# A Fourier mix fed into a gated feed-forward block: the opening cut by residue parity, its transposing writes and reads in two halves

## The chip, the core and the metric

The kernel runs on one core of one Trainium2 chip. The metric is the device time of one execution in microseconds. Engines are named as in the profile: PE (TensorE, matrix products), PEld (its weight loads), DVE (VectorE), ACT (ScalarE), POOL (GpSimd) and SP (SyncE, which here only issues transfers). Every operation of the kernel is recorded through one helper, so every profile line says L25 and the groups are told apart by engine and tile name.

## The reference, cut to what matters

```
x: (8, 3008, 256) float32                       # 8 batches
X = fft(fft(x, axis=1), axis=2).real            # along the sequence, then along the 256 channels
t = X.reshape(24064, 256)
g = t @ w_gate;  v = t @ w_val                  # 256 -> 1536, both
out = (gelu(g) * v) @ w_out                     # 1536 -> 256
```

## The kernel before

**The transforms.** The sequence length is 3008 = 64 x 47. Stage one is a product with a 64-point table `G` for each of 24 row groups `jj`; stage two is a 47-point transform for each of 32 residues `g`. Symmetries of real input halve the work: only half of the outputs, `Y` with 1505 columns in an even plane (`eo` 0) and an odd plane (`eo` 1), is formed for each batch, and the mirrored half is had by a change of sign. The channel transform is folded into the first layer's weights: `gen_w` multiplies each 512-wide column block of `w_gate` and `w_val` by a cosine and sine table `CW` and gives `WE` (even), `WOP` (odd) and `WOM` (odd times minus two).

**Stage one** is `a_step(b, k)`, 12 steps per batch: two products of 256 columns into one PSUM bank, which ACT or DVE copies to `S1`. `z_write` sends `S1` to a buffer `z` in device memory and `z_read` reads it back, transposed, in three thirds into `Ap`. Before stage one, `fold_x` adds and subtracts mirrored channels of the loaded `x`: on DVE for batch 0, on POOL for the others.

**Stage two** is `b_steps(b, eo, q)`: eight products of 47 columns for each quarter `q` of the residues, with `Ap` as weights, and copies from PSUM to `Y`. In batch 0 the odd plane has eight more for its row 0. Stage two of later batches runs in one PSUM bank, `ps_d`, of which there is one; so do most `a_step` and some `gen_w`.

**The main loop** runs over units `u`, 36 for each batch: three chunks of `Y` columns (`CH`: 481, 512, 512 columns) by 12 feed-forward groups of 128. A unit makes the gate and the value for its columns and for the mirrored ones: five first-layer products (`WE`, `WOP`, for the gate also `WOM`), six in the first chunk of batch 0. ACT applies Gelu (`glp`, `glm`), DVE and POOL multiply into `h`. From the end of unit 12 on, eight or six second-layer products (`ps_o`, `Wo_sb`) for the chunk before are run per unit, and `finish` copies and stores their rows.

**The order** of each engine is the program's order, since every engine is wrapped in `_InOrder`: a waiting instruction holds whatever is behind it on its engine. Around the loop the order is written by hand: `extra` (which unit makes which late weight block, casts it on POOL with `cast_w`), `a_first` (which unit makes which stage-one step of batch 1), `first`, `evens` and `later` (stage two of the next batch). In a unit, `fills` are stage-two products put between the unit's own products, two at a time, and `tail` is their copy to `Y`.

**The opening** of batch 0, before unit 0: loads of `x` and of the first weight block; the table `G`; `fold_x` and `a_step` with dummy products (`warm`) between; five `z_write`; three `z_read`; the late weight blocks and batch 1's `x`; the first weight block (`cast_w(0)` on POOL, `gen_w(0, ...)`); the stage-two tables (`cols_t`, `phase_t`, `sin_t`); the load of the Gelu table; dummy products that wait for a small read `gate`; then all eight `b_steps` and unit 0.

The lines that set the order in the units:

```
extra = {1: [lambda: cast_w(1024)], 13: [gen_tf]}
for n, turn in ((0, (ps_o, ps_d, ps_o, ps_d)), (1, (ps_o, ps_o, ps_d, ps_o))):
    for j, bank in enumerate(turn):
        extra.setdefault(4 * n + j, []).append(
            lambda f0=512 + 512 * n, i=1 - j // 2, eo=j % 2, bank=bank: gen_w(f0, i, eo, bank))
a_first = {4: (0,), 5: (1,), 12: (10,), 13: (11,), 14: (12,), 15: (13,)} | {
    8 + j: (2 + 2 * j, 3 + 2 * j) for j in range(4)}
```

Of the kernel before, what the change touches and what calls it, by code (L numbers as in the profile page):

```python
# [9 lines left out]
FP32 = mybir.dt.float32  # L10
# [27 lines left out]
def kernel(  # L38
# [34 lines left out]
    CH = [(1024, NCOL - 1024), (0, 512), (512, 512)]  # L73
    MID = 24
# [26 lines left out]
    lone = const_pool.tile([128, NFC], BF16)  # L101

# [92 lines left out]
    def z_tile():  # L195
        return dram.tile([HJ, 128, C], BF16, tag="z", bufs=2, name="z")
# [14 lines left out]
    def fold_x(b, i, eng, a0=0, an=8, other=None):  # L211
        xt = xins[i]
        o0 = (8 * i + a0) * C
        lo = _sub(xt, [[C, an], [1, 127]], a0 * C + 1)
        hi = _sub(xt, [[C, an], [-1, 127]], a0 * C + 255)
        ea = _sub(xf, [[C, an], [1, 127]], o0 + 1)
        od = _sub(xf, [[C, an], [1, 127]], o0 + 129)
        eng.tensor_tensor(ea, lo, hi, op=ALU.add)
        eng.tensor_tensor(od, lo, hi, op=ALU.subtract)
        (other or eng).tensor_copy(  # L220
            _sub(xf, [[C, an], [128, 2]], o0), _sub(xt, [[C, an], [128, 2]], a0 * C))
# [25 lines left out]
    def cols_t():  # L247
        f4, f8, f16 = (col_q[:, i : i + 1] for i in range(3))
        vec.tensor_scalar(col_q, col_q, MAGIC, None, op0=ALU.add)
        vec.tensor_scalar(col_q, col_q, MAGIC, None, op0=ALU.subtract)  # L250
        vec.scalar_tensor_tensor(col_t, f4, -4.0, col_p, op0=ALU.mult, op1=ALU.add)
        vec.scalar_tensor_tensor(col_bot, f8, -2.0, f4, op0=ALU.mult, op1=ALU.add)
        vec.scalar_tensor_tensor(f8, f16, -2.0, f8, op0=ALU.mult, op1=ALU.add)
        vec.scalar_tensor_tensor(col_j, col_t, 8.0, f16, op0=ALU.mult, op1=ALU.add)
        vec.scalar_tensor_tensor(col_j, f8, 24.0, col_j, op0=ALU.mult, op1=ALU.add)
        vec.tensor_scalar(col_j, col_j, 1.0 / N2, None, op0=ALU.mult)
        for o, b0 in ((0, 0.25), (2 * N2, 0.0)):
            vec.tensor_scalar(
                _sub(quat, [[1, 2 * N2]], o), _sub(col_bot, [[0, 2 * N2]], 0),
                0.25, b0, op0=ALU.mult, op1=ALU.add)  # L260
        vec.tensor_scalar(col_k, col_t, 3.0, None, op0=ALU.is_lt)
        vec.tensor_scalar(col_w, col_k, -TWO_PI, None, op0=ALU.mult)
        vec.tensor_tensor(col_bot, col_bot, col_k, op=ALU.mult)
        vec.tensor_tensor(col_top, col_k, col_bot, op=ALU.subtract)

    TO = 4 * N2
    iota(_sub(rowt, [[2 * N2, 2], [1, 2 * N2]], 0), [[0, 2], [1, 2 * N2]], 0, 0)
    iota(_sub(rowt, [[NJ, 2], [1, MID]], TO), [[0, 2], [1, MID]], 0, 0)
    iota(_sub(rowt, [[NJ, 2], [1, MID - 1]], TO + MID), [[0, 2], [1, MID - 1]], 1, 0)
    pool.memset(_sub(rowt, [[NJ, 2]], TO + NJ - 1), 0.0)  # L270
    pool.memset(_sub(quat, [[1, NJ]], TO), 0.25)
    pool.memset(_sub(quat, [[1, NJ]], TO + NJ), 0.0)
    TG = TO + 2 * NJ
    iota(_sub(rowt, [[NG, 2], [1, NG]], TG), [[0, 2], [-11, NG]], 0, 0)
    pool.memset(_sub(quat, [[1, NG]], TG), 0.25)
    pool.memset(_sub(quat, [[1, NG]], TG + NG), 0.5)
# [59 lines left out]
    def sin_g(i):  # L336
        for h in range(2):
            act.activation(
                _sub(G, [[128, 8], [1, 64]], i * 8 * 128 + h * 64),
                _sub(reds[i], [[64, 8], [1, 64]], 0), AF.Sin, scale=col_h[h][:, :])  # L340

    def turn_g():
        for r, to, of, n, sign in ((0, 0, 0, 16, 1.0), (2, 2, 2, 16, -1.0), (1, 1, 33, 8, 1.0),
                                   (1, 33, 1, 8, -1.0), (3, 3, 35, 8, -1.0), (3, 35, 3, 8, 1.0)):
            pat = [[128, 8], [64, 2], [4, n]]
            act.activation(_sub(G, pat, 16 * 128 + to), _sub(G, pat, of), AF.Copy, scale=sign)
# [44 lines left out]
    def cast_w(f0):  # L391
        big = work.tile([128, 2, NCH, 512], BF16, tag="ev" if f0 == 1024 else "dv", bufs=2, name="wb")
        for i in (1, 0):
            wb[(f0, i)] = big[:, i, :, :]
            pool.tensor_copy(wb[(f0, i)], wst[0][:, i, :, f0 : f0 + 512])

    def gen_w(f0, i, eo, bank):
# [6 lines left out]
        if eo == 0:  # L404
            on_half(ps, act.activation(WE[:, i, fs], ps, AF.Copy))
        else:
            on_half(ps, act.activation(WOP[:, i, fs], ps, AF.Copy))
            on_half(ps, vec.tensor_scalar(
                WOM[:, i, fs], ps, col_m, None, op0=ALU.mult))
# [22 lines left out]
    def n_turn(b):  # L432
        pool.tensor_tensor(
            NA[:, :, :], _sub(Ap, [[0, 2], [C, NG]], 128), TB[:, :, :], op=ALU.mult)
# [27 lines left out]
    def a_step(b, k):  # L462
# [6 lines left out]
        else:  # L469
            ps = ps_o() if b == 1 and k % 2 and 1 < k < 10 else ps_d()  # L470
# [10 lines left out]
    def z_write(b, j0, nj, eng=sync):  # L481
        if "z" not in st[b]:
            st[b]["z"] = z_tile()
        z, S1 = st[b]["z"], st[b]["S1"]
        dst = ap_replace(
            z[0:1, 0, :], ap=[[C, 128], [128 * C, nj], [1, C]], offset=z[j0, 0:1, :].offset)
        eng.dma_start(out=dst, in_=_sub(S1, [[C, nj], [1, C]], j0 * C))

    def z_read(b, third):
        z = st[b]["z"]  # L490
        src = ap_replace(
            z[0:1, 0, :], ap=[[NG * C, 32], [1, NG * C]], offset=z[8 * third, 0:1, :].offset)
        p_step = Ap[:, :, :].ap[0][0]
        dst = ap_replace(
            Ap[:, :, :], ap=[[4 * p_step, 32], [1, NG * C]],
            offset=Ap[:, :, :].offset + third * p_step)
        sync.dma_start(out=dst, in_=src)

    def b_steps(b, eo, q):
# [3 lines left out]
        def mm(gi, m1):  # L503
            def run():
                if "ps" not in box:
                    box["ps"] = ((ps_o, ps_d, ps_vh, ps_vh) if eo else (ps_vh, ps_g) * 2)[q]() \
                        if b == 0 else ps_d()
# [474 lines left out]
```

## Time and profile before

| | |
|---|---|
| median of 3 runs | 631.53 us (631.25 to 631.95) |
| the profiled execution | 629.75 us |
| its span on the core | 627.6 us |
| PE busy | 606.0 us, 97% |
| DVE busy | 541.5 us, 86% |
| ACT busy | 471.8 us, 75% |
| POOL busy | 449.7 us, 72% |
| moved by transfers | 82.39 MB, mean 131 GB/s |

Times in the profile count from the start of the span. In a timeline row the first number is the start, the second how long the row lasts; a group of several instructions in a row overlaps in time where the engine is pipelined. "[x <-A t]" means that the engine sat idle for x before the row and that a result of engine A in tile t ended it. SPq is the queue of SP; its rows are the issuing of transfers, not the transfers. In a table of stretches the columns are the length, then busy time and instruction count of PE, PEld, DVE, ACT and POOL, the granted clock, the share of transfer engines busy and GB/s.

### The profile page before, as it was taken

To read this page: it belongs to the slowest core of one execution; us is meant where nothing else is said; L and a number is where in the kernel's file an instruction comes from. 1 tells how busy PE (TensorE), PEld (TensorE's weight loads), DVE (VectorE), ACT (ScalarE), POOL (GpSimd) and SP (SyncE) were. 2 spreads that over 40 slices of the span, in tenths; PEclk is the share of its full clock that TensorE was granted. 3 is DMA by queue.
4 is the path that set the end of the run, shared out by engine and by line. 5 is a ranking of instruction groups with operands and counts; after the bars stand their busy time and mean duration, and the time that the engine had idled before them with its cause. 6 is when DMAs were issued, how large, how long until landed. Compare 5 with 4: busy or idle time off the path is not lost.

```text
span 627.6 us, 12916 instructions
## 1 busy us (share of the span) xinstructions
PE 606.0 (97%) x4522; PEld 402.0 (64%) x4580; DVE 541.5 (86%) x654; ACT 471.8 (75%) x956; POOL 449.7 (72%) x480
## 2 busy tenths in 40 slices
PE   3899999999999999999999999999999999999997
PEld 2445666766666666766667666666667666666665
DVE  7688988898888998888988898889898898999991
ACT  8687778877788777877778777887778777766662
POOL 8296987769868789687787788687885555556552
PEclk9999999999999999999999999999999999999999
DMA  8997523653237512574246533366223612222113
GB/s 311 348 283 234 153 64 113 173 185 98 76 101 218 194 49 74 177 223 121 51 119 173 190 103 74 104 208 204 56 60 93 194 45 50 60 50 52 39 47 85
DMA packets 65458, 82.39 MB, mean 131 GB/s; under 512 B 8298, under 2 KB 58986, under 8 KB 62578
## 3 DMA queue, kind: packets, MB, share of 16 engines
q1 hardware_dynamic: 63682, 80.65, 42.4%
q0 software_dynamic: 1552, 0.79, 0.9%
q8 instruction: 36, 0.59, 0.4%
q14 instruction: 28, 0.23, 0.1%
q10 hardware_dynamic: 160, 0.13, 0.1%
HBM read 45.08 MB, written 37.25 MB: 131 GB/s over the span
## 4 chain that ended last, share of the span: by engine, by line
PE 91%; DMA 3%; DVE 3%; ACT 1%; issue 1%; POOL 0%; SPq 0%; ACTq 0%; DVEq 0%; POOLq 0%
PE ps_o L25 38%; PE ps_g L25 28%; PE ps_v L25 19%; PE ps_d L25 6%; DMA xin<-in_x_dram 3%; DVE h L25 1%; DVE S L25 0%; DMA z<-S 0%; ACT glp L25 0%; DVE xf L25 0%; ACT glm L25 0%; ACT S L25 0%; POOL xf L25 0%; SPq L25 0%; DVE WOM L25 0%
## 5 line engine op out<-in xcount | busy, mean ns | idle before, releaser
L25 POOL TENSOR_TENSOR h<-glm,dv 128x1024 bf16<-128x1024 bf16 (+1 forms) x138 | 290.9, 2108 | 153.2 <-DVE dv L25 110.0
L25 PE MATMUL ps_o<-Wo_sb,h 128*128 128x256 bf16 x2136 | 277.7, 272 | 0.5 <-DVE S L25 0.3
L25 DVE SCALAR_TENSOR_TENSOR ev<-nq,WN,ps_v 128x512 f32<-128x512 bf16 (+1 forms) x276 | 202.6, 734 | 62.3 <-PE ps_v L25 43.5
L25 ACT ACTIVATE glm<-ps_g 128x512 bf16<-128x512 f32 (+1 forms) x288 | 169.4, 588 | 110.0 <-PE ps_g L25 70.8
L25 PEld LDWEIGHTS <-h 128*128 128x128 bf16 x2208 | 210.8, 97 | 54.6 <-issue 0.9
L25 ACT ACTIVATE glp<-ps_g 128x512 bf16<-128x512 f32 (+1 forms) x288 | 169.9, 590 | 9.9 <-PE ps_g L25 0.3
L25 DVE TENSOR_TENSOR h<-glp,ps_v 128x1024 bf16<-128x1024 bf16 (+2 forms) x150 | 172.9, 1153 | 4.9 <-ACT glp L25 2.7
L25 DVE SCALAR_TENSOR_TENSOR dv<-ev,ps_v 128x1024 f32<-128x1024 f32 (+1 forms) x138 | 164.8, 1194 | 0.0
L25 POOL TENSOR_TENSOR xf<-xin 128x254 bf16<-128x254 f32 x168 | 118.3, 726 | 1.8 <-DMA xin<-in_x_dram 1.8
L25 PE MATMUL ps_g<-Y,WOM 128*128 128x512 bf16 (+1 forms) x288 | 107.7, 374 | 0.3
L25 PE MATMUL ps_v<-Y,WOP 128*128 128x512 bf16 (+1 forms) x288 | 107.7, 374 | 0.0
L25 PE MATMUL ps_v<-Y,WE 128*128 128x512 bf16 (+1 forms) x282 | 105.7, 375 | 0.1
L25 PE MATMUL ps_g<-Y,WOP 128*128 128x512 bf16 (+1 forms) x278 | 103.9, 374 | 1.7
L25 PE MATMUL ps_g<-Y,WE 128*128 128x512 bf16 (+1 forms) x249 | 92.9, 373 | 0.0
L25 PEld LDWEIGHTS <-WOP 128*128 128x128 bf16 x576 | 55.7, 97 | 52.8 <-ACT WOP L25 0.4
L25 PEld LDWEIGHTS <-WE 128*128 128x128 bf16 x576 | 56.0, 97 | 30.9 <-issue 0.6
L25 ACT ACTIVATE osb<-ps_o 128x512 f32<-128x512 f32 x93 | 54.8, 589 | 17.6 <-PE ps_o L25 13.6
L25 PEld LDWEIGHTS <-Ap 128*128 128x128 bf16 (+1 forms) x561 | 40.9, 95 | 33.8 <-issue 0.2
L25 ACT ACTIVATE S<-ps_d 128x512 bf16<-128x512 f32 x80 | 47.4, 593 | 0.1
L25 PEld LDWEIGHTS <-G 128*128 128x128 bf16 x213 | 20.8, 100 | 33.2 <-issue 11.8
L25 ACT ACTIVATE Y<-ps_d 128x192 bf16<-128x192 f32 (+4 forms) x142 | 34.0, 340 | 0.5 <-PE ps_d L25 0.5
L25 PEld LDWEIGHTS <-WOM 128*128 128x128 bf16 x300 | 29.2, 97 | 4.9
(140 smaller groups left out, 262.7 us busy)
## 6 DMA issues: line engine op xcount, KB each, us to landing
out_dram<-osb SPq DMA_DIRECT2D x358, 64.0 KB
xin<-in_x_dram SPq DMA_DIRECT2D x16, 1024.0 KB
Ap<-z SPq DMA_DIRECT2D x24, 512.0 KB
xin<-in_x_dram SPq DMA_DIRECT2D x8, 896.0 KB
z<-S SPq DMA_DIRECT2D x7, 768.0 KB
z<-S SPq DMA_DIRECT2D x8, 512.0 KB
nq<-nrow SPq DMA_DIRECT2D x8, 376.2 KB
z<-S SPq DMA_DIRECT2D x11, 256.0 KB
```

The costliest lines, as they stand in the source:

```text
L25: return lambda *a, **k: self._tc.keep_in_program_order(call(*a, **k))
```

## The change

Residues are handled by parity. `G`'s columns are reordered so that the even residues come out on partitions 0 to 63 of `S1` and the odd ones on 64 to 127. There are two device buffers, `z0` and `z1`, and `z_write` and `z_read` take `halves`. `Ap` holds the 16 even residues first.

In the opening, only the even half is written and read ahead of the loop (five writes of 64 partitions, then three reads); the odd half follows as one write behind the 512 weight block, its reads behind batch 1's first `x` load, and the 1024 block behind these. Only quarters 0 and 1 of stage two run ahead of unit 0. Quarters 2 and 3 (the odd residues) run as fills of units 5 to 8, all in `ps_d`. For batch 0 the first chunk is 512 columns made of even residues alone (`CH0`), the second the 481 columns of both, the third 512 columns of odd residues. Their rows lie two apart in the output, so `store_apart` stores them window by window, and a copy `aside` keeps the columns that would otherwise share a window.

Residue 0 is split into two products of 24 and 23 columns, one in each of quarters 0 and 1, in every batch; the copies to `Y` are two per quarter instead of two to four. In all batches `z` is written and read in two halves.

Other moves: the constants of the channel table are made early on POOL, the small constants of `cols_t` move from DVE to POOL, the single-channel copies of `fold_x` of batch 0 all go to POOL, `cast_w(0)` from POOL to DVE, two copies of first weight blocks from ACT to DVE, `WOM` is made from `WOP` instead of from PSUM; the dummy products between stage-one groups and the `gate` read are gone. The 1024 block is cast three units in, instead of one, its four `gen_w` all use `ps_o`; `load_wo` moves from before the loop to unit 5, `n_first(0)` from unit 0 to unit 8. Stage one of batch 1 runs from unit 8 to unit 17 instead of 4 to 13, and its last read is issued in unit 18 instead of 15.

```
+    CH0 = [(0, 512), (1024, NCOL - 1024), (512, 512)]
...
-    def z_write(b, j0, nj, eng=sync):
+    def z_write(b, j0, nj, halves=(0, 1)):
         if "z" not in st[b]:
-            st[b]["z"] = z_tile()
...
+            st[b]["z"] = [z_tile(half) for half in range(2)]
+        S1 = st[b]["S1"]
+        for half in halves:
+            z = st[b]["z"][half]
+            dst = ap_replace(
+                z[0:1, 0, :], ap=[[C, 64], [64 * C, nj], [1, C]], offset=z[j0, 0:1, :].offset)
+            sync.dma_start(out=dst, in_=_sub(S1, [[C, nj], [1, C]], j0 * C, 64 * half, 64))
...
-                    box["ps"] = ((ps_o, ps_d, ps_vh, ps_vh) if eo else (ps_vh, ps_g) * 2)[q]() \
-                        if b == 0 else ps_d()
+                    box["ps"] = ((ps_o, ps_d) if eo else (ps_vh, ps_g))[q]() \
+                        if b == 0 and q < 2 else ps_d()
...
+        def store_apart(w, t, s):
+            part = lambda p0, n: _sub(t, [[1, C]], s * C, p0, n)
+            if isinstance(w[2], tuple):
+                row, nb = w[2]
+                nc.sync.dma_start(
+                    out=ap_replace(
+                        out, ap=[[64 * C, nb], [2 * C, 16], [1, C]], offset=out.offset + row * C),
+                    in_=part(0, 16 * nb))
...
-        warm((5, 2, 10)[i])
-    z_read(0, 0)
-    z_read(0, 1)
-    gate = work.tile([128, 128], BF16, tag="gate", bufs=1, name="gate")
...
-    z_read(0, 2)
+    warm(7)
+    z_read(0, 0, (0,))
+    z_read(0, 1, (0,))
+    z_read(0, 2, (0,))
     for i in (1, 0):
         load_w(512, i)
+    z_write(0, 0, HJ, (1,))
     load_x(1, 0)
+    for i in range(3):
+        z_read(0, i, (1,))
     for i in (1, 0):
         load_w(1024, i)
...
     for eo in range(2):
-        for q in range(4):
+        for q in range(2):
...
-    load_wo()
-    extra = {1: [lambda: cast_w(1024)], 13: [gen_tf]}
-    for n, turn in ((0, (ps_o, ps_d, ps_o, ps_d)), (1, (ps_o, ps_o, ps_d, ps_o))):
+    extra = {3: [lambda: cast_w(1024)], 5: [load_wo], 13: [gen_tf]}
+    for n, turn in ((0, (ps_o, ps_d, ps_o, ps_d)), (1, (ps_o, ps_o, ps_o, ps_o))):
         for j, bank in enumerate(turn):
-            extra.setdefault(4 * n + j, []).append(
+            extra.setdefault(4 + j if n else (1, 2, 2, 3)[j], []).append(
...
-    a_first = {4: (0,), 5: (1,), 12: (10,), 13: (11,), 14: (12,), 15: (13,)} | {
-        8 + j: (2 + 2 * j, 3 + 2 * j) for j in range(4)}
+    a_first = {8: (0, 1), 9: (2, 3), 18: (13,)} | {10 + j: (4 + j,) for j in range(8)}
...
+    second_half = {5: (0, 2), 6: (0, 3), 7: (1, 2), 8: (1, 3)}
...
+                if b == 0 and i in second_half:
+                    steps, tail, _, _ = b_steps(0, *second_half[i])
+                    fills += steps
```

## The prediction

> **What bounds the kernel now.** I read the page first, then the table of stretches, then the timelines of PE, POOL and SP over the first 75 us, where all that is moved lies.
>
> ```profile
> span 627.6 us, 12916 instructions
> PE 606.0 (97%) x4522; PEld 402.0 (64%) x4580; DVE 541.5 (86%) x654; ACT 471.8 (75%) x956; POOL 449.7 (72%) x480
> ```
>
> ```profile
> 3.50:9.50 6.00, 0.62 (x4) 0.46 (x5) 5.58 (x8) 5.48 (x14) 4.79 (x16) 1.00 1.01 418
> 17.50:18.50 1.00, 0.97 (x4) 0.19 (x2) 0.93 (x6) 0.64 (x2) 0.00 (x0) 1.00 0.96 291
> 36.47:53.30 16.83, 15.30 (x101) 7.76 (x101) 15.51 (x28) 13.54 (x28) 16.83 (x39) 1.00 0.75 196
> 53.30:78.00 24.70, 24.49 (x176) 15.81 (x179) 22.26 (x26) 18.20 (x37) 19.03 (x22) 1.00 0.67 210
> ```
>
> From 53.3 us on PE is full (24.49 of 24.70). So what is won or lost before then, plus any new PE wait behind it, is the whole effect. Loads move 418 GB/s, the transposing writes about 300.
>
> ```profile
> 8.88 0.58 PE L25 MATMUL ps_g<-xf,G 128*128 128x256 bf16 x2 [8.88 <-DVE xf L25]
> 12.46 0.38 PE L25 MATMUL ps_g<-xf,G 128*128 128x256 bf16 x2
> ...
> 23.60 1.90 PE L25 MATMUL ps_d<-G,gate 128*128 128x512 bf16 x8 [2.30 <-DMA gate<-z]
> 28.60 0.38 PE L25 MATMUL ps_v<-Y,WE 128*128 128x481 bf16 x1
> 29.17 0.36 PE L25 MATMUL ps_g<-Y,WOP 128*128 128x481 bf16 x1
> 36.47 0.59 PE L25 MATMUL ps_o<-wb,CW 128*128 128x512 bf16 x2
> 37.70 0.37 PE L25 MATMUL ps_v<-Y,WE 128*128 128x481 bf16 x1
> 53.30 1.03 PE L25 MATMUL ps_o<-Wo_sb,h 128*128 128x256 bf16 x8 [0.25 <-DVE S L25]
> 70.45 0.19 PE L25 MATMUL ps_d<-T0Q,Ap 128*128 128x47 bf16 x2
> ```
>
> The first two rows show the pace of PE (below). The others are my milestones: unit 0 at 28.60, the 1024 block's first product (end of unit 4) at 36.47, unit 5 at 37.70, the first second-layer product (end of unit 12) at 53.30, stage two of batch 1 (unit 21) at 70.45.
>
> ```profile
> 31.77 1.40 POOL L25 TENSOR_TENSOR xf<-xin 128x254 bf16<-128x254 f32 x2 [1.80 <-DMA xin<-in_x_dram]
> 33.25 2.00 POOL L25 CAST wb<-wst 128x1024 bf16<-128x1024 f32 x2
> 35.22 1.40 POOL L25 TENSOR_TENSOR xf<-xin 128x254 bf16<-128x254 f32 x2
> ```
>
> POOL waits for batch 1's first `x` (31.77), folds once, casts the 1024 block by 35.25: just ahead of PE.
>
> ```profile
> 19.88 0.45 SPq L25 DMA_DIRECT2D Ap<-z  x1
> 56.56 0.37 SPq L25 DMA_DIRECT2D z<-S  x1
> 63.50 0.48 SPq L25 DMA_DIRECT2D Ap<-z  x1
> 66.80 1.22 SPq L25 DMA_DIRECT2D xin<-in_x_dram  x2
> ```
>
> The last opening read is issued at 19.88. For batch 1 the last write goes at 56.56, its read at 63.50, three units ahead of need and before the next `x`.
>
> **Part by part: the opening.** DVE's folds end at 13.67 as before. Without dummies the last stage-one copy ends near 16.3 (before 16.65). Then DVE: `reduce_c` 1.7 us (16.56 to 18.22), two casts, `phase_t` 1.4 (20.16 to 21.58). The trace has no DVE cast of 1024 elements: from below, its single-input rows (256 elements 0.32 apart, 512 0.46) extend to 0.74; from above, the fold of 1016 takes 1.22. I take 0.74, the nearer kind; the other end costs 1.0, covered as shown below. `cols_t` on POOL (16 instructions at 0.24, after two 1.8 us memsets) ends near 18.7, beside this. ACT: `sin_t` 1.1, Gelu table 1.3. Half of stage two is 1.7 us on PE. Unit 0's third product comes at about 24.5 instead of 29.17: **a lead of 4.6 us.**
>
> **The lead meets the 1024 block.** PE then needs units 0 to 4: 0.45 us to the end of unit 0, four units of six products of 0.2165 (1.3 us) and four weight blocks of 0.43, and some tenths of waits, so it asks for the 1024 block at 32.3. What POOL has by then depends on batch 1's first `x`. In its queue stand, from 18.8 (first read back, 2 us after issue): three half reads 0.79 MB to 21.0, 1.05 MB of weights to 23.5, the odd write 0.79 MB at 300 GB/s to 26.1, the `x` 1.05 MB at 418 to 28.6. Before, the landing that POOL saw trailed the mean rate by up to 2 us; I take 1.1: 29.7. Bounds: 28.1 (writes overlap reads) and 31.6 (as before). Then come **three** folds of 1.5 us instead of one, and the cast, 1.0: PE resumes at 35.3, unit 5 starts at 35.75. Against 37.70: **-1.95 us**, between -3.5 and -0.05. PE idles 3 us here, so up to 3 us lost or gained in the opening itself changes nothing: this covers the edits there that I cost at zero (casts, `cols_t`, single-channel copies, dummies, `gate`). If the cover were gone, they would cost what they last.
>
> **Units 5 to 12, the odd half in one bank.** PE work: units 5 and 6 with 8 stage-two products (0.2) and a weight block, 1.95 each; unit 7 with 16 (0.6), a block and `gen_wn` (0.6), 2.93; unit 8 with 16 and two stage-one steps of 0.22, 2.34; then 1.74, 1.52, 1.52 and 1.27 up to the first second-layer product: 15.2. The waits come on top. Fills start right behind a unit's value products, while the one `ps_d` still holds the previous quarter. In unit 5 Gelu ends 2.0 after its start; DVE then has two multiplies (0.6 each) queued ahead of the copies to `Y` (0.35 and 0.25 from the 192-element rows of 0.27): free at 3.9. PE is there at 2.4: **1.5**. Unit 7's fills wait for ACT's copies: **0.2**. Behind unit 7, `gen_wn` wants `ps_d` at 8.0 and DVE, again two multiplies first, frees it at 9.6: **1.6**. Unit 8's stage-one step waits for ACT's copies: **0.8**. Sum 19.3; before, 53.30 - 37.70 = 15.6. So **+3.7**, between -0.4 (no wait shows) and +4.5. What is queued behind is all of PE's first layer, and Gelu and DVE behind that. `WOM` from SBUF instead of PSUM (a 264-element row takes 0.29, the old one 0.75) frees DVE, which isn't late at those points.
>
> **Stage one of batch 1.** Five steps instead of one remain behind unit 12: 4 x 0.22 = +0.9. In units 12 to 23 the products are 481 wide instead of 512: 60 x 0.013 = -0.8. Together **+0.1**. Two of its copies now lie on DVE there (1.2 us, DVE has 2.4 idle in 24.7). The last write goes at the end of unit 17 + 0.2; before, such bytes took 2.1 us and 0.6 to be seen. SP then issues two stores, the next `x` and only then the read. The `x` (0.98 MB, 2.3 us) is ahead in the queue; two half reads take 1.5 and 0.5 to land: 7.9 after unit 17. PE wants them after three units of 1.67 and 0.8: 5.8. **+2.1**, between 0.5 and 3.2.
>
> [...]
>
> **All batches.** Two more products in each of 7 batches, at 0.026 (8 take 0.205): **+0.36**. Six more transfers per batch cost SP about 0.5 each, beside long SP waits; from batch 2 on the reads have five units, not three. ACT loses one short copy per plane. `aside` on POOL takes 1.5 (copies of 512 and 256 elements take 0.62 and 0.41) for 1.2 removed, in a unit where POOL waits for DVE anyway. `n_first` at unit 8 has four units for two transfers: they need 3 us each on a quiet queue and come just in time; 7.7 us, what the first waited in the old crowd, would stall PE by up to 4. I take 0 because the transfer engines were only 0.38 busy from 45.5 to 53.3.
>
> **Sum:** -1.95 + 3.7 + 0.1 + 2.1 + 0.36 = **+4.3 us**. The profiled span of 627.6 goes to 631.9, its execution of 629.75 to 634.1; the median, 1.8 above that execution, from 631.53 to **635.8**.
>
> **The rivals.**
> - *Not slower: the one bank costs nothing.* If DVE frees `ps_d` before PE asks (copies done within 1.1 us of the last product, instead of 2.6), the 4.1 us of waits are gone: 631.7. For it: in units 5 to 12 before, DVE was busy 15.5 of 16.8 and PE waited little. Against: the copies stand behind multiplies that wait for Gelu.
> - *The late read lands in time*, if the next `x` doesn't hold it up: 633.7. With the first rival: 629.6, faster.
> - *The clock drops.* PE idles about 3 us in unit 4. The trace shows products at half pace from 8.9 to 12.5 us (a pair of 256 columns every 0.43, later every 0.22), and none such after the idle 2.30 ahead of the `gate` products. If the longer gap brings that pace back for as long, 3.6 us, 1.8 is lost: 637.6. [...]
> - *The lead never arises* (tables late): until 3 us are lost the end is the forecast's.
>
> **How the numbers follow.** Forecast 0.60, one bank free 0.14, read in time 0.12, clock 0.08, both waits gone 0.06. Faster by over 0.2% (1.26 us, about what a measurement of this kernel can tell) is the last case and the lower fifth of the second: 0.09; the rest of the second is within: 0.11; slower 0.80. Range 631.9 to 639.3: below lies 0.13; above, a landing as late as before (+1.9) with both waits at their upper ends, 0.06.
>
> **What would show it.** Right: unit 0 near 24.1; PE idle about 3 us ahead of the 1024 block, ended by POOL's `wb`; waits on DVE's `Y` in units 6 and 7; an idle of about 2 us ahead of batch 1's stage two, ended by the read of `z`. Wrong: a weight block cast before PE asks, second-layer products starting before 53, or no wait at unit 21.

## The result and the profile after

The changed kernel takes 654.39 us (median of four runs, 645.36 to 654.88) against 631.39 us for the kernel before in the same session: a ratio of 1.033, 95% interval 1.024 to 1.042. It is slower, as forecast, but by 23 us where 4.3 were forecast, and far above the range. The profiled execution took 654.52 us. Two single executions of the experiments, one with the dummy products (656.12 us) and one of the mended kernel with the load in unit 5 (640.25 us), fell into a slower state of the chip, and the medians leave them out.

The page's head and busy times of the changed kernel:

```profile
span 652.7 us, 12997 instructions
PE 614.8 (94%) x4581; PEld 403.8 (62%) x4581; DVE 548.9 (84%) x643; ACT 475.5 (73%) x943; POOL 455.8 (70%) x491
```

The span grew by 25.1 us, while PE is busy for 8.8 us more (614.8 against 606.0) with only 59 more products. So PE both waits longer and works more slowly. The milestones of the prediction, in the timeline of PE of the changed kernel:

```profile
25.17 0.61 PE L25 MATMUL ps_v<-Y,WE 128*128 128x512 bf16 x1
37.77 1.01 PE L25 MATMUL ps_o<-wb,CW 128*128 128x512 bf16 x2 [3.83 <-POOL wb L25]
38.58 0.63 PE L25 MATMUL ps_v<-Y,WE 128*128 128x512 bf16 x1
43.69 0.22 PE L25 MATMUL ps_d<-TP,Ap 128*128 128x47 bf16 x2 [0.32 <-DVE Y L25]
53.88 0.58 PE L25 MATMUL ps_v<-Y,WOM 128*128 128x512 bf16 x1 [7.05 <-DVE h L25]
68.97 1.04 PE L25 MATMUL ps_o<-Wo_sb,h 128*128 128x256 bf16 x8
93.60 0.24 PE L25 MATMUL ps_d<-TQ,Ap 128*128 128x47 bf16 x2 [7.05 <-DMA Ap<-z]
```

| stage | before | after | difference | forecast |
|---|---|---|---|---|
| opening, to unit 0 | 28.60 | 25.17 | -3.4 | -4.6 |
| units 0 to 4, to unit 5 | 9.10 | 13.41 | +4.3 | +2.65 |
| units 5 to 12, to the second layer | 15.60 | 30.39 | +14.8 | +3.7 |
| units 12 to 21, to stage two of batch 1 | 17.15 | 24.63 | +7.5 | +2.2 |
| the rest | 557.15 | 559.10 | +1.95 | +0.36 |

(The third forecast is the rest of the prediction's -1.95 for both first rows.) Three idle gaps of PE stand out: 3.83, 7.05 and 7.05 us. Behind each of them the products come at half their pace. The table of stretches of the changed kernel, one stretch behind each gap (length, then busy time and count of PE, PEld, DVE, ACT, POOL, granted clock, transfer share, GB/s):

```profile
37.77:43.40 5.63, 5.60 (x20) 1.90 (x19) 1.58 (x4) 2.36 (x4) 5.30 (x9) 0.50 0.87 320
53.80:60.50 6.70, 6.07 (x57) 2.64 (x57) 3.48 (x10) 1.86 (x4) 0.15 (x2) 0.50 0.01 2
93.60:98.00 4.40, 4.40 (x24) 2.40 (x24) 1.63 (x2) 1.93 (x4) 1.85 (x4) 0.50 0.05 8
```

The granted clock is 0.50 in all three: in the first two, 512-column products start 0.43 us apart, and in the third 481-column ones 0.40, where they start 0.22 and 0.20 apart at a granted clock of 1.00. At full clock the same work would last half of 5.60 + 6.07 + 4.40 us, so 8.0 us are lost to the clock. The opening has a fourth such stretch: from 22.1 to 26.4 us, behind an idle of 1.52 us, the granted clock was 0.60.

What ends the first gap of 7.05 us is a product that waits for DVE, and DVE was held by a single instruction, in its timeline:

```profile
43.55 9.68 DVE L25 TENSOR_SCALAR WOM<-WOP,col_m 128x512 bf16<-128x512 bf16 x1
```

The other five of these products take 0.34 to 0.73 us. POOL at that time, and ahead of it, in its timeline:

```profile
31.56 1.46 POOL L25 TENSOR_TENSOR xf<-xin 128x254 bf16<-128x254 f32 x2 [5.12 <-DMA xin<-in_x_dram]
36.68 1.04 POOL L25 CAST wb<-wst 128x1024 bf16<-128x1024 f32 x1 [0.48 <-DMA wst<-in_moe_w_val_dram]
...
42.09 1.28 POOL L25 DMA_DIRECT2D Wo_sb<-in_moe_w_out_dram  x1
43.39 1.41 POOL L25 TENSOR_TENSOR xf<-xin 128x254 bf16<-128x254 f32 x2
...
52.36 1.44 POOL L25 TENSOR_TENSOR xf<-xin 128x254 bf16<-128x254 f32 x2
```

The first two rows belong to unit 4: `x` landed at 31.56, not at 29.7, and when its three folds were done the weights themselves were still 0.48 us away. The last three rows: POOL issues the `Wo` load and then folds without a gap, and the held product ends at 53.23, within the last fold.

Why the weights were so late stands in the chain of waits of the changed kernel (start, length, what):

```profile
19.82 7.87 DMA z<-S
30.34 6.29 DMA wst<-in_moe_w_val_dram
```

The odd half's write, issued at 19.82, was done at 27.69. SP waited 4.9 us for it with the odd half's reads, and the weights stand behind these in its order: they were issued at 30.34 and landed 6.29 us later. At unit 21, the queue of SP:

```profile
81.63 1.31 SPq L25 DMA_DIRECT2D z<-S  x2
83.04 2.72 SPq L793 DMA_DIRECT2D out_dram<-osb  x2
85.85 1.25 SPq L25 DMA_DIRECT2D xin<-in_x_dram  x2
87.20 1.18 SPq L25 DMA_DIRECT2D Ap<-z  x2
```

The read is issued 5.6 us behind the last write, after two stores and the next `x`, and PE gets its data at 93.60.

### The profile page after: what moved, and what is told of

Its sections match the earlier page's. It is cut to its first block, busy times and chain, and to the rows that moved or that the text cites. A ratio compares the mean times of both kernels' runs of the same rounds, so it can differ in the third digit from the quotient of the medians.

```text
span 652.7 us, 12997 instructions
## 1 busy us (share of the span) xinstructions
PE 614.8 (94%) x4581; PEld 403.8 (62%) x4581; DVE 548.9 (84%) x643; ACT 475.5 (73%) x943; POOL 455.8 (70%) x491
## 4 chain that ended last, share of the span: by engine, by line
PE 89%; DMA 5%; DVE 3%; SPq 1%; ACT 1%; issue 0%; POOL 0%; ACTq 0%; DVEq 0%
PE ps_o L25 37%; PE ps_g L25 28%; PE ps_v L25 18%; PE ps_d L25 6%; DMA z<-S 2%; DVE WOM L25 1%; DMA xin<-in_x_dram 1%; DMA wst<-in_moe_w_val_dram 1%; DMA Ap<-z 1%; SPq L25 1%; DVE h L25 1%; DVE xf L25 0%; ACT glp L25 0%; DVE S L25 0%; SPq L793 0%
## 5 line engine op out<-in xcount | busy, mean ns | idle before, releaser
L25 PE MATMUL ps_v<-Y,WE 128*128 128x512 bf16 (+1 forms) x288 | 109.2, 379 | 0.0
L25 PE MATMUL ps_g<-Y,WOP 128*128 128x512 bf16 (+1 forms) x288 | 108.7, 378 | 0.0
L25 PE MATMUL ps_g<-Y,WE 128*128 128x512 bf16 (+1 forms) x288 | 108.5, 377 | 0.0
L25 PEld LDWEIGHTS <-Ap 128*128 128x128 bf16 (+1 forms) x578 | 45.5, 99 | 58.4 <-issue 22.0
L25 ACT ACTIVATE osb<-ps_o 128x512 f32<-128x512 f32 x93 | 55.2, 594 | 17.8 <-PE ps_o L25 12.8
L25 ACT ACTIVATE Y<-ps_d 128x192 bf16<-128x192 f32 (+4 forms) x133 | 41.5, 408 | 0.7 <-PE ps_d L25 0.7
L25 PE MATMUL ps_d<-xf,G 128*128 128x256 bf16 x166 | 31.8, 273 | 1.6 <-DVE S L25 0.8
```

The source lines that it names most:

```text
L25: return lambda *a, **k: self._tc.keep_in_program_order(call(*a, **k))
```

## The experiments

Each kernel was measured beside runs of the kernel before on the same chip. Since that one's median moved between 630.12 and 631.47 us, I compare the excess over it: +23.0 us for the change.

### What holds DVE's product

**First: the product read from PSUM again.**

```
             if f0:
-                minus_two()
+                on_half(ps, vec.tensor_scalar(
+                    WOM[:, i, fs], ps, col_m, None, op0=ALU.mult))
```

> The changed kernel, with the late minus-two weights (WOM above column 512) read from PSUM again. Theory A (the one 9.68 us product WOM<-WOP on VectorE was held because it reads and writes SBUF while GpSimd issues the Wo load): no WOM takes over 0.8 us, TensorE's 7.05 us wait at 53.88 us goes, and the half-rate stretch at 50 to 60 us (about 3.2 us) goes with it: 654.4 - 10.3 = about 644 us (642 to 647). Theory B (the wait is only passed on, since the longer PSUM reads hold the one bank): 650 us or more, with waits on ps_o in units 3 to 6. Theory C (the clock falls for another reason than this wait): the wait goes and the slow stretch stays, about 647.5 us.

646.62 us, +16.5, in theory A's range. No `WOM` takes over 0.75 us, the 7.05 us wait and the half pace behind it are gone. But the next DVE operation with both sides in SBUF is now the long one, in the timeline of DVE of this kernel:

```profile
49.89 3.16 DVE L25 CAST WN<-WNb 128x12 f32<-128x12 bf16 x1
```

It writes 12 columns. The multiplies into `h`, which read PSUM, ran through the same 10 us at 0.67 to 0.69 us each. So it isn't the product that matters, but that it works from SBUF to SBUF.

**Second: the load three units later.**

```
-    extra = {3: [lambda: cast_w(1024)], 5: [load_wo], 13: [gen_tf]}
+    extra = {3: [lambda: cast_w(1024)], 8: [load_wo], 13: [gen_tf]}
```

> The changed kernel, with the Wo load issued at unit 8 instead of unit 5, when all WOM products are done. Theory A (the Wo load on GpSimd holds the product): all six WOM products under 1 us, 643 to 647 us, unless another SBUF-to-SBUF operation of VectorE near unit 8 is held in its stead for up to 9 us (then 650 to 654 us, and the long operation stands beside the Wo load again). Theory B (GpSimd's folds, which run back to back there, hold it): one WOM product still takes over 5 us, 652 to 655 us.

651.77 us, +21.7. That is within the 650 to 654 us that theory A gave for another held operation, but a `WOM` product was held: the expectation took all products to be done by unit 8's place in POOL's queue, which they weren't. POOL got there at 45.80, ahead of the last product. That gives the clearest pair of rows, DVE first, then POOL, both in their timelines:

```profile
42.78 0.87 DVE L25 TENSOR_SCALAR WOM<-WOP,col_m 128x512 bf16<-128x512 bf16 x1
48.41 4.05 DVE L25 TENSOR_SCALAR WOM<-WOP,col_m 128x512 bf16<-128x512 bf16 x1
```

```profile
45.80 1.28 POOL L25 DMA_DIRECT2D Wo_sb<-in_moe_w_out_dram  x1
...
51.59 1.44 POOL L25 TENSOR_TENSOR xf<-xin 128x254 bf16<-128x254 f32 x2
```

Folds ran at both times. The product ahead of the load got through in 0.87 us, the one behind it was held to 52.46, again within the last fold. In this kernel, the changed one and the one with the product from PSUM, the held operation ends 0.87, 0.87 and 0.74 us behind the start of the last fold, and 6.7 to 11.1 us behind the load's issue. The end follows the folds, not the load.

**Third: one part of the change alone, in the kernel before.**

```
-            on_half(ps, vec.tensor_scalar(
-                WOM[:, i, fs], ps, col_m, None, op0=ALU.mult))
+            if f0:
+                vec.tensor_scalar(WOM[:, i, fs], WOP[:, i, fs], col_m, None, op0=ALU.mult)
+            else:
+                on_half(ps, vec.tensor_scalar(
+                    WOM[:, i, fs], ps, col_m, None, op0=ALU.mult))
```

> The kernel before, with only this part of the change: WOM above column 512 made from WOP in SBUF instead of from PSUM. Theory A (held by the Wo load, which is issued at 28.7 us there and moves its data at about 33 to 43 us): one of the products at 33.0, 36.7, 40.8 us takes several us, and the time goes to 635 to 642 us. Theory B (the folds hold it, or the product is only held at unit 5 of the changed kernel): four products of about 0.35 to 0.7 us, 631 us within 0.7.

630.39 us, ratio 1.000 (0.998 to 1.002): no cost, and theory A in this form (the load in flight is enough) has fallen. The operations of DVE on this tile:

```profile
L25 DVE TENSOR_SCALAR WOM<-WOP,col_m x4: 348/583/945, 35.0 to 45.8; 128x512 bf16<-128x512 bf16 x4
```

The first three ran while `Wo` was still moving (issued at 29.36, landed 15.2 us later), and all four beside folds. What differs is that POOL here runs dry behind the load, 0.42 us ahead of the next fold and 0.82 us behind that one, before its long run of folds begins. New theory: the load must be followed by folds without a gap.

**Fourth: the load behind the last fold.**

```
-    extra = {3: [lambda: cast_w(1024)], 5: [load_wo], 13: [gen_tf]}
+    extra = {3: [lambda: cast_w(1024)], 12: [load_wo], 13: [gen_tf]}
```

> The changed kernel, with the Wo load issued on GpSimd at unit 12, behind the last of its folds, instead of at unit 5, between folds. Theory A (a VectorE operation that works from SBUF to SBUF is held from a Wo load that is directly followed by folds until the folds end): no WOM product and no WN copy above 1 us, TensorE's 7.05 us wait goes; the Wo data lands near 64 us, which is when the first second-layer product can start: 644 to 648 us. Theory B (the folds alone, run back to back, hold it): one WOM product or the WN copy still takes 3 to 10 us, 650 to 655 us.

647.97 us, +17.8, in theory A's range. No `WOM` over 0.91 us: the folds alone hold nothing. PE pays for the late load instead, in its timeline:

```profile
62.37 1.86 PE L25 MATMUL ps_o<-Wo_sb,h 128*128 128x256 bf16 x8 [2.37 <-DMA Wo_sb<-in_moe_w_out_dram]
```

The eight products last 1.86 us, where such a group takes 1.04 at full clock: half pace again, behind a gap of 2.37 us.

**Fifth: both ingredients in the kernel before**, that is, the third experiment and

```
-    load_wo()
-    extra = {1: [lambda: cast_w(1024)], 13: [gen_tf]}
+    extra = {1: [lambda: cast_w(1024)], 5: [load_wo], 13: [gen_tf]}
```

> The kernel before, with the late WOM made from SBUF (no cost by itself) and its Wo load moved behind unit 4's fold, so that folds stand directly ahead of it and behind it. Theory A (load, then folds without a gap, hold VectorE's SBUF-to-SBUF operations until the last fold): one WOM product or the WN copy after about 42 us takes 3 to 8 us, TensorE waits 2 to 6 us for it, 633 to 640 us. Theory B (something else of the changed kernel is needed): no such operation over 1 us, 630 to 632 us.

640.49 us, ratio 1.014 (1.011 to 1.016), just above theory A's range. Timelines of DVE, POOL and PE of this kernel:

```profile
38.59 0.71 DVE L25 TENSOR_SCALAR WOM<-WOP,col_m 128x512 bf16<-128x512 bf16 x1
42.10 9.78 DVE L25 TENSOR_SCALAR WOM<-WOP,col_m 128x512 bf16<-128x512 bf16 x1
```

```profile
40.79 1.24 POOL L25 DMA_DIRECT2D Wo_sb<-in_moe_w_out_dram  x1
...
51.02 1.44 POOL L25 TENSOR_TENSOR xf<-xin 128x254 bf16<-128x254 f32 x2
```

```profile
52.51 0.56 PE L25 MATMUL ps_v<-Y,WOM 128*128 128x480 bf16 x1 [8.37 <-DVE h L25]
```

The same picture without the rest of the change: short ahead of the load, 9.78 us behind it, free within the last fold. The PE wait was 8.37 us, more than the 2 to 6 expected.

**Sixth: POOL made to run dry once behind the load**, by a copy of one column that waits for the product (the copied column is not used).

```
+    extra[5].append(lambda: pool.tensor_copy(lone[:, 0:1], WOM[:, 1, 1024:1025]))
     extra[7].append(gen_wn)
```

> The changed kernel, with one copy on GpSimd behind the Wo load that waits for unit 5's WOM product, so that GpSimd runs dry between the load and the next folds. Theory A (only folds that follow the load without a gap hold VectorE): unit 5's product takes under 1 us, and the WOM and WN of unit 7 under 1 us too: 644 to 648 us. [...] Mixed: unit 5's product is short, unit 7's operation is held by the folds that follow, 646 to 652 us.

646.24 us, +15.9, theory A. DVE, then POOL, in their timelines:

```profile
43.30 0.34 DVE L25 TENSOR_SCALAR WOM<-WOP,col_m 128x512 bf16<-128x512 bf16 x1
48.93 0.96 DVE L25 TENSOR_SCALAR WOM<-WOP,col_m 128x512 bf16<-128x512 bf16 x1
```

```profile
43.71 0.19 POOL L25 COPY lone<-WOM 128x1 bf16<-128x1 bf16 x1 [0.69 <-DVE WOM L25]
```

The load stands where it stood, and the same seven folds follow. One pause of 0.69 us sets DVE free, and the folds behind the pause hold nothing (0.96 and, for the `WN` copy, 0.51 us). So the load alone doesn't hold DVE either, since unit 5's product took 0.34 us while the data was on its way (issued at 41.73, landed 8.8 us later); the unbroken run of POOL behind it does. In the time this gap is worth 23.0 - 15.9 = 7.1 us. That is less than its 7.05 us of wait and 3.0 of half pace, because other waits show once it is gone: 1.29 and 1.51 us on copies to `Y`, and 8.30 instead of 7.05 at unit 21.

Where POOL ran no load directly ahead of its folds, the `WOM` products from SBUF took 0.34 to 0.98 us, so what was held there was less than one fold instruction, 0.7 us (half of the fold row's 1.41). Behind the load the wait was 9.3 us in the changed kernel, through 13 such instructions and six small casts. Why the run behind a load keeps DVE out to its end, no run here shows.

### What delays unit 21

**Stage one of batch 1 two units earlier**, two steps a unit in units 8 to 11 with the second in `ps_o`, the last read in unit 16:

```
-            ps = ps_o() if b == 1 and k in (1, 3) else ps_d()
+            ps = ps_o() if b == 1 and k in (1, 3, 5, 7) else ps_d()
...
-    a_first = {8: (0, 1), 9: (2, 3), 18: (13,)} | {10 + j: (4 + j,) for j in range(8)}
+    a_first = {8: (0, 1), 9: (2, 3), 10: (4, 5), 11: (6, 7), 16: (13,)} | {12 + j: (8 + j,) for j in range(4)}
```

> The changed kernel, with stage one of batch 1 finished at unit 15 instead of 17 (two steps a unit at units 8 to 11) and its last read at unit 16. If the delay of stage one is what makes the wait at unit 21: that wait of 7.05 us falls to 0 to 1 us, the half-rate stretch of 2.2 us behind it goes, and the two steps more a unit cost up to 0.8 us each in two units: 654.4 - 9 + 1 = about 646 us (644 to 648). If something else makes it (the rate of the 64-partition transfers, whenever they start): 4 us or more of the wait stay, 650 us or more.

646.25 us, +16.1: as expected. The last read is issued at 82.32, and PE's first product of that stage runs at 85.75 with no wait. The delay of stage one costs 23.0 - 16.1 = 6.9 us.

**The next `x` behind the read:**

```
-            loads = (0, 14, 19) if b else (8, 12, 18)
+            loads = (0, 14, 19) if b else (8, 12, 19)
```

> The changed kernel, with the third x load of batch 2 issued behind the last z read of batch 1 instead of ahead of it. If the place in the sync queue sets stage two's wait at unit 21: the wait of 7.05 us shrinks by the 1.25 us of the issue and about 2 us of the x transfer to about 3.8 us, and with a gap that short the half-rate stretch at 91 to 98 us (about 2.2 us) may go too: 649 us (647 to 652). If the output stores alone hold the read: the wait stays at 5.8 us or more, the slow stretch stays, 653 us (652 to 654.5).

650.88 us, +20.8, in the first theory's range. In PE's timeline of this kernel:

```profile
90.84 0.21 PE L25 MATMUL ps_d<-TQ,Ap 128*128 128x47 bf16 x2 [2.76 <-issue]
```

The wait is 2.76 us (3.8 expected) and the products behind it run at full pace. The `x` load ahead of the read thus made 4.3 us of the 7.05. For the other 2.76 us the row names no engine; that they are the read itself, issued too late, is argued from the kernel above, where an earlier read leaves no wait.

### What delays unit 5

**The 1024 block's weights ahead of the odd reads and `x`, its cast ahead of the folds:**

```
-    load_x(1, 0)
-    for i in range(3):
-        z_read(0, i, (1,))
     for i in (1, 0):
         load_w(1024, i)
+    for i in range(3):
+        z_read(0, i, (1,))
+    load_x(1, 0)
...
     cast_w(512)
-    extra = {3: [lambda: cast_w(1024)], 5: [load_wo], 13: [gen_tf]}
+    cast_w(1024)
+    extra = {5: [load_wo], 13: [gen_tf]}
```

> The changed kernel, with the weights of the 1024 block loaded ahead of the odd reads and of batch 1's first x, and cast on GpSimd ahead of the folds. If the late landing and the three folds ahead of the cast make the wait of unit 4: the 3.83 us go, the half-rate stretch at 36.6 to 43.4 us (2.6 us) goes, unit 5 starts 4 to 4.5 us earlier, and up to 2.5 us come back as a wait for the odd reads, now behind 1.05 MB of weights: 648 to 651 us while the 9.7 us product at unit 5 stays. Rival (the odd reads or the folds become the bound at once, so the wait only moves): 653 to 656 us.

642.20 us, +12.0, better than either theory. Unit 5 starts at 34.14 without a wait. And because the folds now start later, POOL reaches the `Wo` load only at 46.18, behind all `WOM` products (the last at 43.56) and the `WN` copy (44.76): the held product went as well, by chance. With 7.1 us for that, and if the parts simply add, the wait of unit 4 (the weights' late landing and the folds ahead of their cast) is worth 23.0 - 12.0 - 7.1 = 3.9 us.

**Dummy products in unit 4's gap:**

```
+            if u == 4:
+                warm(14)
```

> The changed kernel, with 14 dummy products added on TensorE at the end of unit 4, where it waits 3.83 us for the 1024 block. If the granted clock falls because of that idle gap: the products of units 5 and 6 (36.6 to 43.4 us) run at their full pace, every 0.22 us instead of 0.43, so the 1024 block still starts at 37.8 us and what follows comes 2 us sooner; but the full pace brings TensorE to unit 6's copies earlier (wait 0.8 to 1.5 instead of 0.32), and unit 5's held product stays: 652 to 654 us. If the clock falls whatever TensorE does there (from load, or from the 2 us of idle that stay): half pace stays in units 5 and 6, 654 to 655 us.

650.72 us, +19.3, below both ranges, but the three executions spread from 644.25 to 651.29, so the time decides nothing. The trace does, in PE's timeline:

```profile
37.18 0.59 PE L25 MATMUL ps_o<-wb,CW 128*128 128x512 bf16 x2 [1.23 <-POOL wb L25]
41.53 0.22 PE L25 MATMUL ps_d<-TP,Ap 128*128 128x47 bf16 x2 [1.41 <-DVE Y L25]
53.04 0.24 PE L25 MATMUL ps_d<-TQ,Ap 128*128 128x47 bf16 x2 [4.60 <-DVE WNb L25]
```

With 1.23 us of idle in place of 3.83 the clock stays at 1.00 from 37.18 to 41, and the pair of 512-column products lasts 0.59 instead of 1.01. So the gap brings the half pace. The other experiments agree: in the first, second, fourth and sixth and in the one with `x` behind the read, unit 4's wait was 2.97 to 3.38 us, and behind it 512-column products took 0.60 to 0.63 us each for some 3 us, where they take 0.38 at full clock (the granted clock of the fourth from 37 to 41 us was 0.66). The faster PE then waits 1.41 us for the copies to `Y`, which the slow one hardly saw (0.32); a later product of DVE is held (5.88 us), and behind the 4.60 us gap the clock falls to 0.50 again.

### Does the change win once this is mended?

**All three mends**, with `Wo` loaded ahead of the folds: the two diffs above (stage one, weights) and

```
     cast_w(512)
-    extra = {3: [lambda: cast_w(1024)], 5: [load_wo], 13: [gen_tf]}
+    load_wo()
+    cast_w(1024)
+    extra = {13: [gen_tf]}
```

> The changed kernel with three mends together: Wo loaded on GpSimd before the folds begin, the weights of the 1024 block loaded and cast ahead of the odd reads, x and folds, and stage one of batch 1 two units earlier. If the three waits (3.83, 7.05 and 7.05 us) and their half-rate stretches (2.6, 3.2, 2.2 us) are the loss: 654.4 - 25.9 = 628.5 us, and with up to 4 us back for transfers that now collide with the Wo load, 627 to 633 us, at or below the kernel before. If the odd half's single bank or the parity order costs by itself: 636 us or more, with waits on the copies to Y.

633.46 us, ratio 1.004 (1.002 to 1.006), just above the 627 to 633 expected. The excess of 23.0 us is down to 3.3; the three parts above add up to 17.9, so they explain most of it, and their meeting saves 1.8 us more. What is left, in PE's timeline:

```profile
36.77 0.21 PE L25 MATMUL ps_d<-TP,Ap 128*128 128x47 bf16 x2 [1.64 <-DMA Ap<-z]
40.27 0.22 PE L25 MATMUL ps_d<-TP,Ap 128*128 128x47 bf16 x2 [1.41 <-DVE Y L25]
45.97 0.75 PE L25 MATMUL ps_d<-CW,wb 128*128 128x1 bf16 x24 [1.52 <-DVE Y L25]
49.27 0.39 PE L25 MATMUL ps_d<-xf,G 128*128 128x256 bf16 x2 [0.74 <-ACT Y L25]
```

The last three are the one-bank waits of the prediction.

**The load back in unit 5**, behind all of DVE's SBUF operations, in this kernel:

```
-    load_wo()
     cast_w(1024)
-    extra = {13: [gen_tf]}
+    extra = {5: [load_wo], 13: [gen_tf]}
```

> The kernel with the three mends (633.46 us), with only the Wo load back between the folds at unit 5. If the early Wo load takes the odd reads' bandwidth: the 1.64 us wait at unit 5 goes. The load now stands behind the WOM products but ahead of the WN copy: by theory A that copy is held for 3 to 10 us, and with it VectorE's multiplies; the time is then 633 to 640 us. By theory B (no hold): 631 to 632.5 us.

632.97 us, ratio 1.0023 (1.0009 to 1.0037). The 1.64 us wait is gone, so the early load had delayed the odd reads. Nothing was held, which doesn't speak against theory A: the `WN` copy ended at 45.42, 0.05 us ahead of the load's issue at 45.47. The gain is small because the clock fell in one stretch (below); the four executions with a granted clock of 0.997 or more took 630.75 to 631.69 us.

**The copies of the odd half on ACT**, and `WN` made in unit 9 in `ps_o` (the bank in `gen_wn`), on top of that:

```
-            if b or (eo if q < 2 else q % 2):
+            if b or q >= 2 or eo:
...
-        ps = ps_d()
+        ps = ps_o()
...
-        vec.tensor_copy(WN[:, :], WNb[:, :])
+        act.activation(WN[:, :], WNb[:, :], AF.Copy)
...
-    extra[7].append(gen_wn)
+    extra.setdefault(9, []).append(gen_wn)
```

> The kernel with the three mends (633.46 us), with the Wo load back between the folds at unit 5, which then comes behind all WOM products; the second half's copies to Y all on ScalarE instead of half on VectorE; WN made at unit 9 in the other bank, its last copy on ScalarE. If VectorE's copies behind its multiplies are what PE waits for in units 6 and 8: 1.41 falls to 0.2 to 0.8, the 1.52 ahead of WN goes, the 1.64 for the odd reads goes with the early Wo load: 633.5 - 3.9 = about 629.6 us (628.5 to 631.5), at the kernel before. If ScalarE becomes the bound in its stead: 632 us or more, with waits on its copies of 1.5 us or more.

631.84 us, ratio 1.0014 (0.9998 to 1.0030): not to be told from the kernel before, between the two cases expected. The waits on copies to `Y` are gone, but the next ones take their place, in PE's timeline (of the longest of the twelve executions, 634.47 us):

```profile
47.55 0.39 PE L25 MATMUL ps_o<-xf,G 128*128 128x256 bf16 x2 [1.11 <-POOL xf L25]
...
56.97 1.05 PE L25 MATMUL ps_o<-Wo_sb,h 128*128 128x256 bf16 x8 [1.73 <-DMA Wo_sb<-in_moe_w_out_dram]
```

Now POOL's folds are late, since batch 1's `x` was put last.

**That version with `load_wo` in unit 2:**

```
-    extra = {5: [load_wo], 13: [gen_tf]}
+    extra = {2: [load_wo], 13: [gen_tf]}
```

> The version with the copies on ScalarE (ratio 1.0014 to the kernel before), with the Wo load issued behind the second fold instead of the fifth. The load is then issued near 43 us and lands near 52 us: the 1.73 us wait of the first second-layer product goes; the waits for folds (0.74, 1.11, 0.93, 1.08 us) stay or grow by up to 1 us in all, as more folds stand behind the load: 630 to 631.5 us, 0.998 to 1.001 of the kernel before. If the last WOM product (41.96 us there) slips behind the load it is held for many us: above 636 us.

631.79 us, ratio 1.0020 (1.0006 to 1.0034), just above the range expected. The `Wo` wait is gone, one wait for a fold is left, and still it is no faster.

**And with `x` first again, the 1024 weights second, the odd reads last**, the product from PSUM, the cast in unit 1, the load in unit 4 (on the changed kernel, with the stage-one mend and the copies on ACT):

```
     load_x(1, 0)
-    for i in range(3):
-        z_read(0, i, (1,))
     for i in (1, 0):
         load_w(1024, i)
+    for i in range(3):
+        z_read(0, i, (1,))
...
-    extra = {3: [lambda: cast_w(1024)], 5: [load_wo], 13: [gen_tf]}
+    extra = {1: [lambda: cast_w(1024)], 4: [load_wo], 13: [gen_tf]}
```

> The version with the copies on ScalarE, with batch 1's first x ahead of the 1024 weights and these ahead of the odd reads, the cast behind the first fold, the late WOM from PSUM and the Wo load behind the fourth fold. If late folds are what is left of the loss: the waits for folds (3.9 us) and for Wo (1.7 us) go, and 1.5 to 3 us come back as waits for the 1024 block and the odd reads at units 4 to 5: 627.5 to 630.5 us, 0.994 to 0.999 of the kernel before. If the collisions of the loads decide: waits of 3 us or more at units 4 to 5, with the half pace behind them, 632 us or more.

632.06 us, ratio 1.0030 (1.0017 to 1.0042). Neither case: waits at units 4 to 5 are small (0.35 and 0.54 us), those for folds and `Wo` nearly gone (0.29), yet it isn't faster than the kernel before. So the lead is lost elsewhere. The table of stretches shows where, units 5 to 12, first the version with the load in unit 2, then the kernel before:

```profile
34.06:54.00 19.94, 16.77 (x146) 8.63 (x144) 13.80 (x24) 15.38 (x34) 15.20 (x29) 1.00 0.81 242
```

```profile
37.70:53.30 15.60, 14.49 (x98) 7.37 (x97) 14.28 (x26) 12.37 (x25) 15.60 (x36) 1.00 0.72 191
```

Unit 5 starts at 34.16, 3.5 us ahead of the kernel before. But PE is busy for 16.77 us up to the second layer instead of 14.49: 2.3 us of the lead were work moved behind unit 4, the 48 products of the odd half of stage two (of stage one there is less there, 18 products against 22). Another 2 are waits there (0.74, 1.11 and 1.09 us against at most 0.25). Units 12 to 21 take 18.44 instead of 17.15 us, 1.13 of it in one wait behind DVE's `ev`, which itself waited 2.41 us for the load of the row `nq`. The odd half has its part in this too, since `nq` is made from it in `n_first`, now in unit 8:

```profile
56.54 0.36 PE L25 MATMUL ps_v<-Y,WOP 128*128 128x481 bf16 x1 [1.13 <-DVE ev L25]
```

(That row is of the version with the load in unit 2, in PE's timeline.) The rest takes 557.10 against 557.15 us. So -3.5 + 4.2 + 1.3 = +2.0 us, against 1.9 us between the spans (629.5 and 627.6). Half pace in the opening (512-column products of 0.61 to 0.63 us from 25.03 to 26.28 us in the version with the load in unit 2) isn't what keeps it back: its three executions at a clock of 1.00 took 630.94 to 631.62 us, and the kernel before 629.64 to 629.85 at that clock. No version that I ran beats the kernel before.

## Why the prediction was right or wrong

The direction held, and so did the kind of wait at four places (the opening, the 1024 block, the one bank, unit 21). The size failed, by 19 us, since the largest loss was in a term taken at nothing.

- **The opening** was nearly right: unit 0 at 25.17 (24.1 forecast). `cols_t` on POOL ended at 21.62, not 18.7: DVE's `phase_t` waited 2.06 us for it, ACT's tables 2.51 us, and PE's stage two 1.52 us for these. With the dummies gone, stage two and unit 0 then began at half pace (0.60 from 22.1 to 26.4 us). The working had left such losses to the cover of the wait in unit 4, and that wait, 3.83 us, did cover them.
- **The lead meets the 1024 block** was right in kind and short in two terms. `x` landed at 31.56, on the upper bound of 31.6 instead of the 29.7 taken. And the working asked only when POOL would be free; the weights, held in SP's queue behind the odd reads, landed at 36.68. The odd write, counted to 26.1, was done at 27.69. PE started at 37.77, 2.5 us later than forecast.
- **"WOM from SBUF instead of PSUM ... frees DVE"** is the step that failed. It was given as a gain worth nothing; it cost a 7.05 us wait of PE and 3.0 us of half pace behind it. Taken away alone it gives back 7.1 us. I priced the operation by its width and didn't ask what else works from SBUF at that moment. The move of `load_wo` between the folds was a second edit costed at nothing without a cover being named. The first costs nothing alone (1.000 in the kernel before). With the move and the product from PSUM, only the `WN` copy was held, 3.16 us, and PE has one wait more than with the load behind the folds, 0.81 us. Together they cost, in the kernel before as well (+9.0 us).
- **The odd half in one bank** was right in place and size, and hidden: 1.5, 0.2, 1.6 and 0.8 us forecast; 1.41, none flagged, 1.52 and 0.74 seen once the held product was gone. In the changed kernel the half-pace PE met less of it (0.32, 0.44, 0.74).
- **Unit 21** was right in kind: stores and the next `x` ahead of the read. The term was 2.1 us and measured 7.05. From the last write's issue to the data it took 12.0 us, where 7.9 from the end of unit 17 were counted: the working gave SP's issue of the two stores nothing (2.72 us), and the read took 6.27 us from its issue to landing by the chain of waits. The second rival fails with it: with the next `x` behind the read, 2.76 us of wait were left, where it had none.
- **The clock** was a rival at 0.08 with 1.8 us, seen in one place. It fell behind each of the three gaps and took 8.0 us, besides the opening. The gap forecast at 3 us lay between two of the kernel before, 2.30 us with full pace behind it and 8.88 us with half pace, and with `x` later it would be longer: the chance should have been one half or more.
- **All batches**, +0.36, is not seen: 557.10 against 557.15 us in the version with the load in unit 2. `n_first`, taken at 0 within it, shows once the large waits are mended, in the 1.13 us above. The +1.95 of the changed kernel there is the half pace at 93.6 to 98 us (2.2).

What no run separates is why the excess of the parts (17.9) and of the rest (3.3) leaves 1.8 us of the 23.0; and why one of the four runs took 645.36 us: that is where the kernels without the held product lie, but no profile of it was taken.

## What to carry to other kernels

Price an edit that moves an operand from PSUM to SBUF, or a load into the middle of POOL's work, by what POOL does at that moment, not by its width (the same 512 columns took 0.35 us and 9.68 us here); and where a long hold shows, look for the run of POOL instructions that ends with it, and break that run. A lead in the opening is only worth what isn't deferred work: count what the next stage is given before counting the lead, and follow what lands last in the queue of transfers, not only what the waiting engine has to do. Count a gap of some 3 us on PE as two costs, the wait and the slower products behind it: in the timelines of PE that I read here every gap of 2.97 us or more, up to 8.88, had both.

## What the runs showed of the hardware that was not expected

- A DVE operation from SBUF to SBUF was held while POOL ran without a pause behind a transfer that it had issued itself: one of 512 columns took up to 9.78 us (0.35 without the hold), one of 12 columns 3.16 us. The multiplies of DVE that read PSUM were not held (0.67 to 0.69 us each). With one pause of POOL of 0.69 us the product took 0.34 us. Beside folds without such a load ahead, or with a load followed by a pause, such an operation took 0.98 us at most.
- The half pace doesn't need one gap of 3 us. A gap of 2.37 us brought it (`Wo` load in unit 12) and one of 2.76 us (load in unit 8), while another of 2.76 us (`x` behind the read) and one of 2.30 us (the kernel before) did not. In the mended version with the load in unit 5 no gap from unit 5 to 61 us was longer than 1.51 us, and still, in the table of stretches:

```profile
40.00:44.00 4.00, 2.46 (x25) 1.04 (x24) 3.17 (x7) 2.53 (x6) 4.00 (x10) 1.00 0.30 115
44.00:48.00 4.00, 4.00 (x46) 2.07 (x46) 0.92 (x4) 1.19 (x2) 3.98 (x6) 0.57 0.67 205
```

PE was busy for 2.46 of 4 us, and the clock of the next stretch fell to 0.57. The version with the early load had the same wait, 1.52 us, and kept 1.00. So below 2.97 us the length of one gap didn't decide it; in this stretch PE idled for 1.51 us at most at a time, and it came all the same. What decides it there, no run here shows.
